# Block-sparse attention and a low-rank mixer with an MLP: two heads' scores side by side, the mask as a product, crossbar transposes, a fixed order

## The chip, the cores and the metric

The kernel runs on one core of a Trainium2 chip. The metric is device microseconds for one execution. Executions are labelled fast or slow by the granted clock and the spread of times, and comparisons use fast runs alone. The profiles are of one execution each. In them PE is TensorE (matmuls), PEld its weight loads, ACT ScalarE, DVE VectorE, POOL GpSimd, and SP the engine that issues most DMAs. A DMA's landing is the time from its issue until all of its data has arrived.

## The reference

Four batches, eight heads, 768 positions, head size 64. Attention sees only some 32-blocks of keys; the result, as 768 x 512 per batch, goes through a rank-32 mixer over the positions and an MLP with 2048 hidden units.

```python
scores = scale * np.matmul(q, k.transpose(0, 1, 3, 2))
mask = np.abs(blk_i - blk_j) <= 1                       # neighbours
mask |= (blk_i == 0) | (blk_j == 0) | (blk_i == n_blocks - 1) | (blk_j == n_blocks - 1)
# ... and three sampled key blocks for each query block
attn = softmax(np.where(mask, scores, -1e9))
x = np.matmul(attn, v)                                  # to (batch, 768, 512)
h = x.transpose(0, 2, 1) @ U @ V
u = x + h.transpose(0, 2, 1)
out = u + np.maximum(u @ w_ch1, 0.0) @ w_ch2
```

## The kernel before

A pair of heads is the unit of work: 16 pairs, four per batch. TensorE transposes q and k. Each head has an augmented q and k of 128 rows: 64 of data and 64 that carry the mask (one-hot blocks on one side, a bias on the other), so that one 128-row product gives masked scores. The exponential runs on ScalarE from PSUM. The MLP of a batch is cut into steps that are dealt out between the score steps of the next batch.

```python
def load_v(b, hp):                       # called at the start of the pair that uses it
    ld = ldpool.tile([P, 2, T, D], FP32, tag="ldv", name="vld")
    nc.sync.dma_start(out=ld, in_=v[b, 2 * hp : 2 * hp + 2].rearrange(...))
    nc.gpsimd.tensor_copy(out=vts[b % 2][:, 2 * hp : 2 * hp + 2, :, 0:D], in_=ld)
# ...
def attn_front(i, st):                   # 12 transposes a pair on TensorE, 4 copies on VectorE
    for s_, aug in zip(st, (qaug, kaug)):
        pstp = pst_tile([P, S], FP16)
        for t in range(T):
            nc.tensor.transpose(out=pstp[:, t * P : (t + 1) * P], in_=..., identity=id16)
        for h in range(2):
            nc.vector.tensor_copy(out=aug[i % NAUG][h][drows[h], :], in_=pstp[drows[h], :])

def attn_scores(i, h, g):                # one head, one key tile: 128 rows, data and mask
    for c in range(2):
        nc.tensor.matmul(psc[:, c, 0:HS], kT[:, g * P : (g + 1) * P],
                         qT[:, c * HS : (c + 1) * HS], start=True, stop=True)
    nc.scalar.activation(out=est..., in_=psc[:, :, 0:HS], func=AF.Exp, scale=0.125)
# ...
def ut(cc):                              # u = x + h, transposed on TensorE, per batch
    # 3 products with the identity and one with the mixer's V, copied by ScalarE
# ...
(load_rest, load_w1, load_mix, load_w2)[hp]()   # weights, in batch one, from GpSimd's queue
```

The scheduler is free to order the instructions of an engine.

The softmax here doesn't subtract the row's maximum and nothing guards it: scores larger than these inputs give would overflow.

## Time and profile before

| | before |
|---|---|
| time, median of two runs | 355.55 us (355.48 to 355.61) |
| TensorE busy, granted clock | 91%, 0.989 |
| batch one (no MLP beside it) | 65.4 us |
| a period with attention and MLP | 80.4 us |
| last MLP alone | 51.5 us |

The lines are shown and read in the prediction below. A windows line has the window, its length, the busy us and count of PE, PEld, DVE, ACT and POOL, the granted clock, the DMA share and GB/s. A line of groups has the place in the code, the engine, what is written from what, the shape, the count, then busy us and mean ns of one, then the idle time in front of it and what ended it. A line number may be that of a helper: after the change all matmuls have the same one, so tile names tell them apart.

### The profile page before, as it was taken

To read this page: it belongs to the slowest core of one execution; us is meant where nothing else is said; L and a number is where in the kernel's file an instruction comes from. 1 tells how busy PE (TensorE), PEld (TensorE's weight loads), DVE (VectorE), ACT (ScalarE), POOL (GpSimd) and SP (SyncE) were. 2 spreads that over 40 slices of the span, in tenths; PEclk is the share of its full clock that TensorE was granted. 3 is DMA by queue.
4 is the path that set the end of the run, shared out by engine and by line. 5 is a ranking of instruction groups with operands and counts; after the bars stand their busy time and mean duration, and the time that the engine had idled before them with its cause. 6 is when DMAs were issued, how large, how long until landed. Compare 5 with 4: busy or idle time off the path is not lost.

```text
span 354.7 us, 6743 instructions
## 1 busy us (share of the span) xinstructions
PE 321.5 (91%) x2803; PEld 189.5 (53%) x2803; DVE 118.5 (33%) x233; ACT 185.5 (52%) x292; POOL 62.5 (18%) x97
## 2 busy tenths in 40 slices
PE   1698882899999999899999999989999999999995
PEld 0356561465756445465756445565756445566442
DVE  3703441034525112324535112325435112244211
ACT  1589993478494431678594431587584432433000
POOL 2519931312303001111202001102101001000000
PEclk9999999799999999999999999999999999999999
DMA  7999999404121111302021211000000011000021
GB/s 236 350 232 229 250 263 291 148 3 133 34 102 55 67 70 52 118 2 89 5 87 27 94 59 61 31 0 3 2 0 2 32 59 61 30 2 0 30 91 59
DMA packets 20874, 30.67 MB, mean 86 GB/s; under 512 B 2444, under 2 KB 17228, under 8 KB 20844
## 3 DMA queue, kind: packets, MB, share of 16 engines
q1 hardware_dynamic: 17184, 25.89, 22.0%
q0 software_dynamic: 3472, 4.24, 7.1%
q8 instruction: 22, 0.36, 0.4%
q10 hardware_dynamic: 188, 0.11, 0.1%
q14 instruction: 8, 0.07, 0.1%
HBM read 28.19 MB, written 6.29 MB: 97 GB/s over the span
## 4 chain that ended last, share of the span: by engine, by line
PE 62%; ACT 16%; DMA 6%; issue 5%; DVE 5%; POOL 5%; ACTq 0%; POOLq 0%; DVEq 0%
PE ps L350 23%; PE ps L333 17%; ACT est L259 13%; PE psc L253 10%; PE ps L273 6%; DMA vld<-in_v_dram 5%; PE ps L238 2%; ACT tT L341 1%; PE ps L348 1%; PE ps L305 1%; DMA small<-small_const 1%; POOL w2t L226 1%; POOL vt_97 L143 1%; POOL vt_98 L143 1%; POOL stqld L133 1%
## 5 line engine op out<-in xcount | busy, mean ns | idle before, releaser
L259 ACT ACTIVATE est<-psc 128x768 f16<-128x768 f32 x192 | 146.4, 826 | 86.0 <-PE psc L253 84.9
L350 PE MATMUL ps<-w2t,tT 128*128 128x512 f16 x384 | 87.3, 379 | 0.0
L333 PEld LDWEIGHTS <-w1t 128*128 128x128 f16 x512 | 48.9, 98 | 33.1 <-DVE q1aug_102 L244 0.7
L343 DVE TENSOR_SCALAR tT<-ps 128x384 f16<-128x384 f32 x64 | 35.7, 558 | 89.5 <-PE ps L333 84.5
L350 PEld LDWEIGHTS <-tT 128*128 128x128 f16 x384 | 37.5, 98 | 43.7
L341 ACT ACTIVATE tT<-ps 128x384 f16<-128x384 f32 x64 | 32.6, 509 | 40.6 <-PE ps L333 29.2
L273 PEld LDWEIGHTS <-est 128*128 128x128 f16 x1152 | 45.6, 98 | 14.6 <-ACT est L259 5.9
L288 POOL CAST xh<-xf 128x384 f16<-128x384 f32 x32 | 16.3, 510 | 197.9 <-DVE xf L282 197.9
L357 DVE TENSOR_TENSOR of<-xf,ps 128x512 f32<-128x512 f32 x24 | 16.5, 688 | 81.1 <-PE ps L350 81.1
L273 PE MATMUL ps<-vt_97,est 128*128 128x65 f16 x576 | 28.3, 196 | 1.8 <-ACT est L259 1.5
L253 PE MATMUL psc<-q0aug_99,k0aug_105 128*128 128x384 f16 x72 | 18.3, 356 | 4.6 <-DVE k0aug_105 L244 2.1
L273 PE MATMUL ps<-vt_98,est 128*128 128x65 f16 x576 | 21.0, 193 | 1.1 <-ACT est L259 0.9
L280 DVE RECIPROCAL rcp<-ps 128x6 f32<-128x6 f32 x32 | 6.2, 194 | 39.3 <-PE ps L273 39.3
L253 PE MATMUL psc<-q1aug_100,k1aug_106 128*128 128x384 f16 x72 | 17.4, 340 | 1.7 <-ACT est L259 1.5
L282 DVE TENSOR_TENSOR xf<-ps,rcp 128x384 f32<-128x384 f32 x32 | 17.8, 558 | 1.2
L253 PE MATMUL psc<-q1aug_104,k1aug_110 128*128 128x384 f16 x60 | 13.5, 325 | 1.6 <-ACT est L259 1.5
L253 PE MATMUL psc<-q1aug_102,k1aug_108 128*128 128x384 f16 x60 | 13.5, 325 | 1.3 <-ACT est L259 1.2
L305 PE MATMUL ps<-xh,Ut 128*128 128x512 f16 x24 | 7.3, 440 | 7.8 <-POOL xh L288 7.8
L253 PE MATMUL psc<-q0aug_103,k0aug_109 128*128 128x384 f16 x60 | 13.5, 325 | 0.9 <-ACT est L259 0.4
L253 PE MATMUL psc<-q0aug_101,k0aug_107 128*128 128x384 f16 x60 | 13.9, 333 | 0.4 <-ACT est L259 0.2
L133 POOL CAST stkld<-kld 128x768 f16<-128x768 f32 x16 | 13.3, 831 | 5.3 <-DMA kld<-in_k_dram 5.3
L133 POOL CAST stqld<-qld 128x768 f16<-128x768 f32 x15 | 12.5, 831 | 7.5 <-issue 5.4
(106 smaller groups left out, 365.9 us busy)
## 6 DMA issues: line engine op xcount, KB each, us to landing
qld<-in_q_dram SPq DMA_DIRECT2D x16, 384.0 KB, 4.7
kld<-in_k_dram SPq DMA_DIRECT2D x16, 384.0 KB, 4.0
vld<-in_v_dram SPq DMA_DIRECT2D x16, 384.0 KB, 3.5
out_dram<-of SPq DMA_DIRECT2D x24, 256.0 KB, 2.0
w1t<-in_moe_w_ch_dram POOLq DMA_DIRECT2D x4, 512.0 KB, 11.0
w2t<-in_moe_w_ch_dram POOLq DMA_DIRECT2D x4, 512.0 KB, 13.2
oh<-onehot_const ACTq DMA_DIRECT2D x1, 96.0 KB, 3.9
q0aug_99<-onehot_const SPq DMA_DIRECT2D x1, 96.0 KB, 4.1
```

Of the source, the lines that this page charges most:

```text
L133: last = eng.tensor_copy(out=st.rearrange("p t h d -> p h t d"), in_=ld)
L253: nc.tensor.matmul(psc[:, c, 0:HS], kT[:, g * P : (g + 1) * P], qT[:, c * HS : (c + 1) * HS], start=True, stop=True,)
L259: nc.scalar.activation(out=est.rearrange("k (c n) -> k c n", c=2), in_=psc[:, :, 0:HS], func=AF.Exp, scale=0.125,)
L273: nc.tensor.matmul(pav[:, j, h, :], ests[h][g][:, sc * P : (sc + 1) * P], vt[:, 2 * hp + h, g, 0 : D + 1], start=(g == 0), stop=(g == T - 1),)
L282: nc.vector.tensor_tensor(out=xs.rearrange("p j (h d) -> p j h d", h=2), in0=pav[:, :, :, 0:D], in1=rcp[:, :, :, None].broadcast_to([P, 3, ...
L288: nc.gpsimd.tensor_copy(out=xh[:, 3 * c : 3 * c + 3, hp * P : (hp + 1) * P], in_=xs)
L305: nc.tensor.matmul(pa, Ut[:, sc, :], xh[:, sc, :], start=(sc == 0), stop=(sc == T - 1))
L333: nc.tensor.matmul(pt, w1t[:, cc, jj * P : (jj + 1) * P], uT[cc][:, c * HS : (c + 1) * HS], start=(cc == 0), stop=(cc == NCC - 1),)
L341: nc.scalar.activation(out=dst, in_=pt, func=AF.Relu)
L343: nc.vector.tensor_scalar_max(out=dst, in0=pt, scalar1=0.0)
L350: nc.tensor.matmul(pch, tT[jj][:, sc * P : (sc + 1) * P], w2t[:, jj, :], start=False, stop=(jj == NJJ - 1),)
L357: nc.vector.tensor_add(out=of, in0=xf[:, sc, :], in1=pch)
```

## The change

The intent is to take work off TensorE, the bound.

1. **Row pairs.** Two heads' data lie in rows 0 to 63 and 64 to 127 of one tile, and two 64-row products run side by side.
2. **Mask.** In batch one it is added by a second 64-row pair of products. From batch two on it is a 0/1 product on VectorE after the exponential.
3. **Mixer per pair** in place of per batch, so that u is ready pair by pair.
4. **Crossbar.** q and k from the third pair on, and all of u, are transposed by DMA; the crossbar stands for this DMA transpose.
5. **Fixed order.** Every engine keeps program order; loads run two pairs ahead; filler (the MLP's steps, put between the score steps) is dealt out by stated costs.

```diff
+def turn_dma(sts):
+    for st, nm in zip(sts, "qk"):
+        tt = qkpool.tile([P, T, P], FP16, tag=nm + "T", name=nm + "T")
+        keep(nc.sync.dma_start_transpose(out=tt, in_=st.rearrange("p t h d -> p (t h d)")))
 ...
+def scores(i, g, c, est, on_pe):
+    for h in range(2):
+        mm(psc[:, h, 0:HS], kT[rows[h], kc], qT[rows[h], qc], True, not on_pe)
+    if on_pe:
+        for h in range(2):
+            mm(psc[:, h, 0:HS], kb[rows[h], kc], oh[rows[h], qc], False, True)
+    keep(nc.scalar.activation(out=est[:, c], in_=psc[:, :, 0:HS], func=AF.Exp, scale=0.125))
+def mask_mul(g, est):
+    keep(nc.vector.tensor_tensor(out=est, in0=est, in1=m01[:, g]...broadcast_to(...), op=ALU.mult))
 ...
+for i in range(HP):                                   # batch one
+    for g in range(T):
+        # scores, values two steps late ...
+        if g == 0: sts[i + 2] = load_qk(i + 2, cast)  # SP load, then GpSimd cast, in order
+        if g == 1: load_v(i + 2)
+        if g == 2:
+            if i == 1: load_w1()
+            if i == 3: load_w2()
+        if g == 3: qkT[i + 1] = turn_pe(sts.pop(i + 1)) if i < 1 else turn_dma(sts.pop(i + 1))
 ...
+FILL = 2.2
+for i in range(HP, NPAIR):                            # batches two to four
+    for g in range(T):                                # a "slot"
+        # two score steps, the mask product of the slot before, then
+        spent += finish_pair(prior, g)                # values in slots 1, 2; mixer in 3, 4, 5
+        if hp == 0 and b > 1 and g == 5: fill.extend(mlp_steps(b - 1))
+        run_fill(FILL - spent)
+        # load_qk in slot 0, load_v in slot 1, turn_dma in slot 3
```

## The prediction

> **What bounds the kernel now.** I read the page first: TensorE is busy for 91% of the span at a granted clock of 0.99, ScalarE for 52%, VectorE for 33%.
>
> ```profile
> PE 321.5 (91%) x2803; PEld 189.5 (53%) x2803; DVE 118.5 (33%) x233; ACT 185.5 (52%) x292; POOL 62.5 (18%) x97
> ```
>
> I then cut the span where the chain of waits changes its character, with the windows view (columns: window, its length, then busy us and count for PE, PEld, DVE, ACT and POOL, granted clock, DMA share, GB/s).
>
> ```profile
> 0.00:65.40 65.40, 42.85 (x459) 27.47 (x460) 22.25 (x49) 41.37 (x55) 32.55 (x50) 0.96 0.98 259
> ...
> 75.50:155.90 80.40, 78.01 (x708) 46.12 (x705) 28.23 (x56) 45.12 (x74) 13.24 (x20) 1.00 0.21 70
> ...
> 303.20:354.70 51.50, 47.31 (x268) 25.01 (x266) 14.44 (x24) 11.02 (x24) 0.00 (x0) 0.99 0.10 36
> ```
>
> There are three kinds of stage. Until 65 us TensorE idles a third of the time and the DMA share is 0.98: batch one's attention has no MLP yet to fill it. Then come three periods of 80.4 us in which attention of one batch and the MLP of the one before share TensorE, busy 97%. Last comes the MLP of batch four alone, 51.5 us.
>
> The chain of waits (start, length, work) gives the rates and batch one's stall:
>
> ```profile
> 43.59 12.76 DMA vld<-in_v_dram
> ...
> 57.27 4.65 DMA vld<-in_v_dram
> ...
> 252.85 2.28 PE ps L273 x72
> ...
> 307.81 20.97 PE ps L333 x128
> ...
> 329.00 3.45 PE ps L350 x16
> 332.67 3.45 PE ps L350 x16
> ```
>
> A matmul's listed duration (326 ns for 384 columns) contains its pipeline, so I use starts. First MLP product: 20.97/128 = 0.164 us. Second: (332.67-329.00)/17 = 0.216 us. Probability times values: 2.28/72 = 0.032 us. In the timeline six transposes take 0.50 us with a tail of about 0.17, so 0.055 each, and four score matmuls take 0.81 us in all, so 0.163 each. The first two lines show batch one waiting 12.76 + 4.65 = 17 us for V, which is on its way beside the weight loads.
>
> The grouped rows price the rest:
>
> ```profile
> L259 ACT ACTIVATE est<-psc 128x768 f16<-128x768 f32 x192 | 146.4, 826 | 86.0 <-PE psc L253 84.9
> ...
> L343 DVE TENSOR_SCALAR tT<-ps 128x384 f16<-128x384 f32 x64 | 35.7, 558 | 89.5 <-PE ps L333 84.5
> ...
> L282 DVE TENSOR_TENSOR xf<-ps,rcp 128x384 f32<-128x384 f32 x32 | 17.8, 558 | 1.2
> ```
>
> Back to back an exponential costs 146.4/192 = 0.763 us, and it spends 85 us waiting for scores: ScalarE isn't the bound outside batch one.
>
> [...] Only start-up has a change: after the two 24-row mask matmuls (0.82 us from 8.14) the 128-row transposes start 0.11 us later than 384 columns at the cold rate (0.32 us) allow. That is weak evidence for some 0.1 us. [...]
>
> **The change part by part**, TensorE time per batch in the steady stage. Before: 96 scores x 0.163 = 15.6; 288 values x 0.032 = 9.1; 48 transposes of q and k x 0.055 = 2.6; six 512-column mixer products 1.3; the u-transposes, 24 x 0.055 + 8 x 0.163 = 2.6; 128 x 0.163 = 20.8; 102 x 0.216 = 22.0. Sum 74.0 of the 80.4.
> - Scores: a head needs only 64 rows once the mask rows leave the product. Two heads side by side make 48 steps of 0.163 in place of 96: -7.8. In batch one the mask is still added by a second 64-row pair, so nothing is saved there.
> - The crossbar takes all but two q/k transposes and all u-transposes off TensorE: -2.6 and -2.6. The mixer becomes 24 + 24 products of 128 columns, 2.6, in place of 1.3 plus the six in the second MLP product, 1.3: nothing.
> - Sum 61.0 per batch: 13.0 less, 39 over three batches.
> - VectorE: 24 mask products of 1536 elements, [...] +23.0. Mixer adds 8 x 0.56 and four small casts, +5.7. Gone are 16 copies of 0.55 and one cast, -9.5. From 28.2 it goes to about 47: beside TensorE's 61, off the path.
> - ScalarE loses eight u-copies of about 0.55: from 45.1 to about 41.
> - The fixed order deals out 2.2 us of filler, mixer and value work per slot of two score steps, so a slot is about 2.2 + 2 x 0.163 = 2.53 us on TensorE against 2 x 0.763 + about 1.3 x 0.51 = 2.2 on ScalarE.
>
> Now the time, stage by stage. **Batch one:** first exponential at about 12 us as before (12.61), 48 x 0.8 = 38.4, since ScalarE binds there. V is fetched two pairs ahead, so the 17 us wait goes; but the crossbar transposes of pairs three and five are queued just behind w1 and w2 loads (11 and 13 us to landing each), for which I add 6. End at 57. **72 slots:** scores 144 x 0.163 = 23.4; values of 11 pairs 25.1; mixer 8.0; MLP 3 x 41.5 less about 9 that the slots don't reach = 115.5. Sum 172. Two mode switches a slot at 0.1 (chosen from the weak evidence): 14.4. Counting the code's stated costs (41.7 a batch against 2.2 a slot), the filler is empty in about five slots, which then last the exponentials' 1.55: +4.5. Twice the MLP of a batch is queued in the very slot in which its last transpose is issued, so TensorE waits for add, cast and crossbar, about 4 each (add and cast 1.1 from rows of that kind, a small DMA 2 to 3 by the landing times of before): +8. The opening of batch two +2, plain gaps as before (80.4 - 78.0 a batch) +7. Sum 208. **Tail:** last pair's values and mixer 3.0, left-over MLP 9, the last MLP 41.5, output 3.7: 57. In all 57 + 208 + 57 = 322 us, against 355.6.
>
> **Rivals.** *The row pairs don't overlap, or the switches are dear.* Without overlap +0.163 x (144 + 96) = +39, less what batch one hides behind ScalarE: about 350, no gain. With switches of 0.2 us instead of 0.1: +14, 336. [...] *The crossbar is the new wait:* if a 192 KB transpose takes 6 us or more, two of them no longer fit in the three slots (7.6 us) before their use: +1 to 3 us a pair, 335 to 350. DMA is idle (share 0.2) after batch one, which speaks against; in batch one it is the likeliest loss. *Everything is hidden anyway:* with free switches and quick transposes, 300.
>
> **Range and chances.** The range 303 to 341 runs from free switches and transposes to 0.2 us a switch with a slow crossbar. To land above 348 both TensorE terms must fail together. Chances: faster 0.93, same 0.05, slower 0.02.
>
> **What would show it.** Right: steady batches of 65 to 69 us; two score matmuls starting within some ns of each other; mask products near 0.96 us; batch one over near 57; TensorE waits of about 4 us near the start of batches three and four; a last stage of about 57. The prediction would be wrong most of all if score pairs start 0.16 us apart, if gaps of 0.2 us stand at each change between 64 and 128 rows, if mask products last 1.8 us, or if TensorE waits for transposes in every pair.

## The result

| | before | changed |
|---|---|---|
| median of two runs | 355.55 us (355.48 to 355.61) | 375.14 us (373.28 to 377.01) |
| granted TensorE clock | 0.989 | 0.904 |

The ratio is 1.054, with a 95% interval of 1.041 to 1.067: the changed kernel is slower by 5%, where 322 us and a gain were forecast. A ratio here is the mean time of one kernel's fast runs over that of the other's of the same rounds, so it is not quite the ratio of the medians that I quote.

The page of the changed kernel, busy times and the slices of TensorE, its clock and the DMA (40 slices of 9.4 us):

```profile
PE 307.9 (82%) x2759; PEld 155.8 (42%) x2759; DVE 173.8 (46%) x298; ACT 175.8 (47%) x258; POOL 89.9 (24%) x129
...
PE   1985078850799999795699997987899999999995
...
PEclk9999559585589999999599999998899999999999
DMA  7816944299390044438340906264802011210011
```

TensorE's busy time fell only from 321.5 to 307.9 us, and it now idles for 67 us. There are two holes in batch one, and the clock is at half in and after them. The windows view, cut where batches begin:

```profile
0.00:93.00 93.00, 51.84 (x555) 24.74 (x555) 21.86 (x51) 38.73 (x50) 29.91 (x49) 0.80 0.67 145
93.00:167.00 74.00, 69.41 (x578) 33.83 (x580) 43.33 (x69) 42.95 (x64) 19.54 (x26) 0.89 0.41 112
167.00:241.10 74.10, 63.64 (x627) 33.30 (x628) 44.10 (x73) 42.99 (x64) 21.36 (x29) 0.93 0.44 111
241.10:317.10 76.00, 69.73 (x658) 35.37 (x658) 46.02 (x75) 43.28 (x64) 16.18 (x23) 0.96 0.33 79
317.10:375.20 58.10, 53.28 (x349) 28.59 (x346) 18.53 (x33) 7.86 (x16) 2.91 (x5) 1.00 0.14 48
```

Batch one takes 93.0 us, where 57 was predicted (+36). The 72 slots take 224.1, where 208 was (+16). The tail takes 58, where 57 was. That is the whole miss of 53 us. The waits view of the changed kernel (who waited for whom, total us, times, longest) names three new waits of TensorE, for kT (k transposed), xh (x in float16, which the mixer reads) and uT (u transposed), and the wait of GpSimd that stands behind the one for xh:

```profile
POOL qst L140 <- DMA qld<-in_q_dram: 33.7, 8, 6.1
...
PE psc L104 <- DMA kT<-kst: 28.4, 3, 14.5
...
PE pa L104 <- POOL xh L331: 15.1, 15, 3.6
PE pt L104 <- DMA uT<-uh: 7.8, 3, 4.0
```

**The wait for k.** The timeline of SP, the DMA-issuing engine (start, duration of the issue, what):

```profile
30.48 1.32 SPq L378 DMA_TRANSPOSE uT<-uh  x1
31.85 1.78 SPq L181 DMA_TRANSPOSE qT<-qst  x1
33.68 10.20 SPq L181 DMA_TRANSPOSE kT<-kst  x1
43.92 0.58 SPq L132 DMA_DIRECT2D qld<-in_q_dram  x1
```

The w1 load was issued at 30.40. The transpose of k behind it lands 14.5 us after its issue; even the issue takes 10.20 us, and the loads of the pair after next stand behind it. The DMA view from 38 to 42 us, in the midst of the w1 load (queue, packets, MB, share of 16 engines; q0 has the weights, q1 what SP issued):

```profile
q0 software_dynamic: 218, 0.77, 95.1%
q1 hardware_dynamic: 219, 0.05, 11.0%
```

The same from 86 to 90 us, in the w2 load:

```profile
q0 software_dynamic: 629, 0.63, 92.2%
q1 hardware_dynamic: 626, 0.15, 29.6%
```

And from 60 to 64 us, where three transposes run with no weights beside them:

```profile
q1 hardware_dynamic: 2400, 0.59, 65.5%
```

In the two windows beside a load both queues moved the same number of packets, 218 to 219 and 629 to 626, as if they took turns. A packet of the weight load holds 3.5 KB (0.77 MB/218) or 1.0 KB; a packet of the transpose holds 0.24 KB. So the transpose crawls there at one packet for each of the other's, and the load with the smaller packets lets through three times as much of it (0.15 against 0.05 MB; 0.59 MB with no load beside it). Not every microsecond is so even: from 34 to 36 us the view has 82 packets against 534, which nothing here explains. The trace shows what equal counts cost the side with the small packets: the transpose of k behind w1, 192 KB, lands in 14.5 us, where the quickest of k takes 2.6 and of u 2.5. The hold of the issue shows in the w2 load too: 4.31 us for the transpose of k issued at 78.81, where that of pair four took 1.24. In the prediction I looked up only how long the loads take.

**The clock.** From 40 to 50 us TensorE is busy for 1.83 us and the granted clock is 0.50, and it stays low for part of the next 60 us (0.67 from 50 to 110 us). After the second hole too it is 0.50, from 93 to 98 us. So the holes of 14.5 and 12.6 us go with half clock. But the clock also fell after far shorter pauses: from 62.0 to 65.4 us TensorE's longest is 1.36 us, a wait for k, and half clock follows for 10 us.

```profile
62.00:65.40 3.40, 2.04 (x26) 0.86 (x25) 1.29 (x4) 1.61 (x3) 0.00 (x0) 1.00 0.61 123
65.40:75.60 10.20, 9.02 (x74) 4.11 (x74) 3.66 (x8) 4.39 (x7) 4.57 (x8) 0.50 0.28 103
```

A wait of 1.47 us before 156.41 is followed by half clock too (0.50 from 157.6 to 160.9 us); one of 1.72 us before 232.99 is not (1.00 from 233 to 238 us). So these traces give no length of pause from which the clock falls. The first two slots after the first hole, those of pair three, last 4.3 and 3.4 us; those of pair two lasted 3.2 and 1.6.

**The wait for xh.** GpSimd's timeline in pair eight (start, duration, what, idle before it):

```profile
153.15 0.83 POOL L140 CAST qst<-qld 128x768 f16<-128x768 f32 x1 [5.99 <-DMA qld<-in_q_dram]
154.36 0.83 POOL L140 CAST kst<-kld 128x768 f16<-128x768 f32 x1 [0.38 <-DMA kld<-in_k_dram]
155.13 1.23 POOL L331 CAST xh<-xs 128x384 f16<-128x384 f32 x1
```

In the fixed order the cast of q for a later pair stands ahead of the cast of x, which the mixer needs now. It idles 5.99 us for its load, which was itself late: SP issued it at 149.70, behind an output store that had to wait for VectorE. The first product of the mixer then starts at 156.41, after 1.47 us of idle TensorE, and such waits come again in pairs nine, twelve and thirteen.

```profile
156.41 0.33 PE L104 MATMUL pa<-xh,Ut 128*128 128x128 f16 x3 [1.47 <-POOL xh L331]
```

**What was as forecast.** The timeline of PE in batch one:

```profile
30.12 0.33 PE L104 MATMUL psc<-oh,kb 64*128 64x384 f16 x2
30.38 0.35 PE L104 MATMUL pav<-vt,est 128*128 128x65 f16 x6
30.66 0.34 PE L104 MATMUL psc<-qT,kT 64*128 64x384 f16 x2
30.84 0.33 PE L104 MATMUL psc<-oh,kb 64*128 64x384 f16 x2
```

Two products of 384 columns take the time of one, and the next pair starts 0.18 us later: the row pairs overlap. From the 64-row pair at 30.12 to the 128-row product at 30.38 are 0.26 us, 0.10 more than the 0.16 that 384 columns take. Over all 67 changes each way between 110 and 320 us the median cost is 0.098 us into 64 rows and 0.095 out, computed from start to start, less the columns at that rate. The groups that answer to those of before:

```profile
L301 ACT ACTIVATE est<-psc 128x768 f16<-128x768 f32 x192 | 145.3, 809 | 108.9 <-PE psc L104 108.7
...
L308 DVE TENSOR_TENSOR est<-est,m 128x1536 f16<-128x1536 f16 x72 | 71.8, 997 | 0.7 <-ACT est L301 0.6
```

A mask product takes 997 ns for 1536 elements, where 960 was forecast. At the pace of VectorE's float32 rows from PSUM in the kernel before (384 elements in 558 ns, 512 in 688, so 1.02 ns an element and 168 ns besides) I estimate 1.7 us.

### The profile page after: what moved, and what is told of

Read it like the earlier page. It is cut to its first block, busy times and chain, and to the rows that moved or that the text cites.

```text
span 375.2 us, 6642 instructions
## 1 busy us (share of the span) xinstructions
PE 307.9 (82%) x2759; PEld 155.8 (42%) x2759; DVE 173.8 (46%) x298; ACT 175.8 (47%) x258; POOL 89.9 (24%) x129
## 5 line engine op out<-in xcount | busy, mean ns | idle before, releaser
L104 PE MATMUL pt<-uT,w1t 128*128 128x384 f16 x512 | 96.0, 341 | 7.8 <-DMA uT<-uh 7.8
L104 PE MATMUL pch<-w2t,tT 128*128 128x512 f16 x384 | 92.1, 388 | 0.0
L104 PE MATMUL psc<-qT,kT 64*128 64x384 f16 x384 | 58.3, 355 | 29.9 <-DMA kT<-kst 28.4
L308 DVE TENSOR_TENSOR est<-est,m 128x1536 f16<-128x1536 f16 x72 | 71.8, 997 | 0.7 <-ACT est L301 0.6
L402 ACT ACTIVATE tT<-pt 128x384 f16<-128x384 f32 x64 | 31.5, 492 | 55.7 <-PE pt L104 55.2
L404 DVE TENSOR_SCALAR tT<-pt 128x384 f16<-128x384 f32 x64 | 35.6, 557 | 46.6 <-PE pt L104 45.7
L104 PE MATMUL pav<-vt,est 128*128 128x65 f16 x1152 | 50.5, 197 | 0.0
L373 POOL CAST uh<-xf 128x384 f16<-128x384 f32 x32 | 20.9, 656 | 98.7 <-DVE xf L369 57.9
L331 POOL CAST xh<-xs 128x384 f16<-128x384 f32 x32 | 20.4, 636 | 71.4 <-DVE xs L324 67.9
L321 DVE RECIPROCAL rcp<-pav 128x6 f32<-128x6 f32 x32 | 6.2, 195 | 40.8 <-PE pav L104 40.6
L140 POOL CAST qst<-qld 128x768 f16<-128x768 f32 x15 | 12.7, 846 | 51.8 <-DMA qld<-in_q_dram 33.7
L104 PE MATMUL pa<-xh,Ut 128*128 128x128 f16 x96 | 11.0, 239 | 15.4 <-POOL xh L331 15.1
L104 PE MATMUL psc<-oh,kb 64*128 64x384 f16 x96 | 19.7, 385 | 0.5 <-ACT kb L242 0.5
```

The costliest lines, as they stand in the source:

```text
L104: nc.tensor.matmul(out, lhsT, rhs, start=start, stop=stop, skip_group_check=loose)
L140: keep(cast[nm].tensor_copy(out=st.rearrange("p t h d -> p h t d"), in_=ld))
L308: nc.vector.tensor_tensor(out=est, in0=est, in1=m01[:, g].rearrange("p (c n) -> p c n", c=2)[:, :, None, :] .broadcast_to([P, 2, 2, HS]), ...
L321: keep(nc.vector.reciprocal(out=rcp, in_=pav[:, :, :, D]))
L331: keep(nc.gpsimd.tensor_copy(out=xh[:, 3 * c : 3 * c + 3, :], in_=x3))
L373: keep(nc.gpsimd.tensor_copy(out=uh[:, 3 * c : 3 * c + 3, :], in_=u3))
```

## The experiments

All kernels were correct. "Before" was run beside each, 354 to 358 us. There are four runs of each kernel (two of the changed one), and times are medians of them; the ratios leave out one slow run each of E2 and E11 (the medians of their fast runs are 348.8 and 323.0). The two runs of the changed kernel lie 3.7 us apart, so a difference from it carries some 2 us of doubt.

| kernel | us | ratio to before (95%) |
|---|---|---|
| changed | 375.1 | 1.054 (1.041 to 1.067) |
| E1: q, k of pairs one to five on TensorE | 353.2 | 0.993 (0.987 to 0.998) |
| E2: weight loads apart | 349.4 | 0.980 (0.975 to 0.985) |
| E3: casts late | 364.6 | 1.026 (1.023 to 1.030) |
| E4: filler 1.85 and 2.1 | 371.8 | 1.044 (1.038 to 1.049) |
| E5: E1 + E3 + E4 | 334.4 | 0.942 (0.935 to 0.948) |
| E6: E5, mask on TensorE | 346.7 | 0.973 (0.968 to 0.978) |
| E7: E5, all q, k on TensorE | 341.0 | 0.958 (0.953 to 0.962) |
| E8: changed, order free | 355.9 | 1.002 (0.998 to 1.006) |
| E9: E5 + E2 | 327.1 | 0.919 (0.914 to 0.924) |
| E10: E9, order free | 348.8 | 0.981 (0.977 to 0.986) |
| E11: E9, casts last, filler 1.8 and 2.15 | 323.4 | 0.908 (0.903 to 0.912) |

### E1: transposes of batch one back on TensorE

```diff
-qkT[i + 1] = turn_pe(sts.pop(i + 1)) if i < 1 else turn_dma(sts.pop(i + 1))
+qkT[i + 1] = turn_pe(sts.pop(i + 1)) if i < HP else turn_dma(sts.pop(i + 1))
```

> Only batch one is changed: q and k of its pairs (and of pair five) are transposed on TensorE again, the u transposes stay on the crossbar. Theory A (the crossbar's 256-byte packets take turns with the weight loads' packets of 1 to 4 KB, so transposes last as long as the weight load): TensorE's waits of 14.5 and 12.6 us for k go, and with them the half clock after them; batch two starts near 60 us in place of 93, total near 342 us. Rival B (whatever queues behind the weight loads waits, so the wait moves to the q, k and v loads): the fourth or fifth pair then waits 10 us or more for a load, total 355 to 375.

353.2 us, 22 less. Both long waits for k are gone and batch two starts at 66.6 us in place of 93.0. It isn't the 60 us expected, and the total is 11 us above theory A's 342, because waits of other kinds are left in batch one: TensorE waits 2.2 us at 51.3 for xh, whose cast stands on GpSimd behind a cast of q that waits for its load; the granted clock falls to 0.54 from 50 to 60 us; and the first four slots of pair four last 4.9, 3.4, 3.0 and 4.0 us. TensorE's longest wait for a transpose from 48 to 90 us is 2.1 us, for u of pair four. The wait of 10 us that rival B asks for isn't seen; GpSimd's longest wait for a load there is 5.6 us.

### E2: weight loads apart from the transposes

```diff
-if g == 2:
-    if i == 1: load_w1()
-    if i == 3: load_w2()
+if g == 2 and i == 0: load_w1()
+if g == 0 and i >= 2: load_w2(i - 2)          # a quarter each
 ...                                            # and the same in pairs five and six
```

> The crossbar does what it did, but the weight loads are issued where few transposes are in flight: w1 in pair one, w2 in four pieces at the start of pairs three to six. Theory A: the k transposes land within 6 us, no wait over 3 us in batch one, total 340 to 350 us. Rival C (two 192 KB crossbar transposes in a row are too slow for a short pair by themselves, with or without weights): waits of 8 us or more before pairs three and five stay, total above 365 us.

349.4 us, 26 less, with the crossbar doing all that it did. The time to landing of the k transposes (minimum, median, maximum of 14), first in the changed kernel:

```profile
DMA to landing us min/median/max: 2.6/5.8/14.5
```

In E2:

```profile
DMA to landing us min/median/max: 2.6/4.9/6.7
```

The longest wait of TensorE for k is 2.5 us; the longest landing is a little over the 6 us expected. (The profiled execution is one labelled slow, 352.4 us, the other three are 346.8 to 350.0; I use it for the landings and this wait alone.) Theory A holds and C falls: the crossbar is quick enough by itself; what cost the time here was running for long beside a load with larger packets (14.5 us to landing there, 6.7 at most in E2). E1 and E2 take away either side of the same collision and gain about the same.

### E3: casts after what the mixer needs

```diff
-sts[i + 2] = load_qk(i + 2, cast)             # slot 0: load and cast; after stores and filler
-load_v(i + 2)                                  # slot 1
+sts[i + 2] = load_qk(i + 2, cast, casts)      # at the start of slot 0: load alone
+load_v(i + 2, casts)
+if g == 4:
+    while casts: casts.popleft()()             # the casts, in slot 4
```

> Batch one's waits stay. q, k and v of the pair after next are requested at the start of a pair before anything else, and their casts stand in GpSimd's fixed order in slot five, after the casts of x that the mixer needs. Theory D (in the fixed order a cast that waits for its load holds the cast of x behind it, and TensorE waits for that one): TensorE's 12 us of waits for xh in pairs eight to thirteen fall below 2 us, total 8 to 11 us less, near 365 us. [...]

(The expectation counts slots from one, the code from zero.)

364.6 us, 10.6 less, in the waits view:

```profile
POOL qst L141 <- DMA qld<-in_q_dram: 1.0, 1, 1.0
...
PE pa L104 <- POOL xh L335: 6.1, 10, 1.4
```

GpSimd's wait for q falls from 33.7 to 1.0 us, TensorE's for xh from 15.1 to 6.1. In batches two to four those over 0.45 us sum to 2.5; below 2 was expected. The total came as expected. Theory D holds. The mask products aren't the main cause of these waits: they are all still there. They do lengthen the casts (686 ns beside them, 509 without, in E5 and E6). The waits for u, which this edit was not meant for, grow from 7.8 to 10.7 us.

### E4: less filler in a slot

```diff
-run_fill(FILL - spent)                         # 2.2
+run_fill((1.85 if i < 9 else 2.1) - spent)
```

(A plain 1.85 could not be built: too much filler was left over, and a tile of an older batch was still held by it.)

> Batch one's waits stay. One number is changed: the filler dealt out per slot is 1.85 us up to pair nine and 2.1 us after, in place of 2.2, so that filler of the batch before is left when the next batch's is queued. Theory E (TensorE waits 2.9 and 4.0 us for the last u transpose because the filler has run out, and the clock falls to half after it): both waits vanish, slots of 9.2 and 8.2 us become 2.5, total 8 to 12 us less, near 365 us. Rival: the work only moves to the last stage, total the same.

371.8 us, 3.3 less, which isn't clear of the noise (1.044, 1.038 to 1.049, against 1.054, 1.041 to 1.067), where 8 to 12 were expected. The waits for the last u transpose fall from 7.8 to 1.5 us and the slots of 9.2 and 8.2 us become 2.4 and 3.3, as theory E has it. But the waits for xh grow from 15.1 to 19.9 us and the slot with the mixer's first product takes up to 8.3 us. So waits of another kind grew where these went.

### E5: the three together

> The three edits together: q and k of pairs one to five transposed on TensorE, casts late, filler 1.85 and 2.1. If the three causes are separate (crossbar beside weights -22 us measured, xh casts behind loads -10.6, filler -3.3 measured), the total is 375 - 36 = 339 us; if the filler's gain was masked by the xh waits that grew in its place, some 6 us more comes off: 330 to 335. Rival: the gains overlap and the total stays above 345.

334.4 us, 40.8 less than the changed kernel; the three alone sum to 36. So the edits help each other by some 5 us, and the total is in the range of the second expectation. That it is E4's gain, hidden behind the waits that E3 takes away, fits E4's longer waits for xh and E3's longer ones for u, but no run of two of the edits shows it. This version beats both kernels: the change's arithmetic is worth its price once these waits are gone.

### E6: the mask on TensorE in all batches

```diff
-scores(i, g, c, est, False)
-if g > 0: mask_mul(g - 1, ests[g - 1])
+scores(i, g, c, est, True)
```

> The three edits, with the mask added on TensorE by a second 64-row pair in all batches and no product on VectorE. If the row pairs and the product are worth what the prediction said (144 steps of 0.163 us), this is 20 to 25 us slower than the three edits alone. Rival: VectorE's product holds up TensorE elsewhere [...] and gives half of it back: 5 to 12 us slower.

346.7 us, 12.4 more than E5: between the two expectations, nearer the rival's. TensorE has 144 steps of 0.163 = 23.5 us more to do, so half of what the product saves is lost again. A part is seen in the windows view from 93 to 263 us; E5 first, then E6:

```profile
93.00:263.00 170.00, 164.33 (x1664) 86.15 (x1662) 119.09 (x193) 112.06 (x167) 56.49 (x70) 0.99 0.47 108
```

```profile
93.00:263.00 170.00, 170.00 (x1802) 90.61 (x1801) 57.46 (x119) 106.55 (x156) 40.96 (x67) 1.00 0.40 107
```

With VectorE at 57 us in place of 119 and GpSimd at 41 in place of 56, TensorE doesn't idle at all; in E5 it idles 5.7 us. Over all 72 slots it idles 15.7 us in E5 and 8.7 in E6, so some 7 of the 11 us lost are idle time; the rest I have not settled.

GpSimd's share is a result of its own. Its casts of x, E5 first, then E6:

```profile
L335 POOL CAST xh<-xs 128x384 f16<-128x384 f32 x32 | 21.9, 686 | 100.5 <-DVE xs L328 100.5
```

```profile
L335 POOL CAST xh<-xs 128x384 f16<-128x384 f32 x32 | 16.2, 509 | 124.9 <-DVE xs L328 124.9
```

Without the mask products a cast is back at the 510 ns of the kernel before, so it is they that cost it some 177 ns; by what means the traces don't show.

### E7: q and k of all pairs on TensorE

```diff
-qkT[i + 1] = turn_dma(sts.pop(i + 1))          # batches two to four
+qkT[i + 1] = turn_pe(sts.pop(i + 1))
```

> The three edits, with q and k of all pairs transposed on TensorE, so that the crossbar turns u only. If the crossbar is free outside batch one, TensorE's 11 x 12 x 0.055 = 7 us more show in full: 6 to 8 us slower than the three edits alone. Rival: the crossbar's transposes hold up loads on the in-order queue also in the later batches; then it is the same or faster.

341.0 us, 6.7 more: the 11 x 12 x 0.055 = 7 us of transposes show in full. Outside batch one the crossbar is free, as predicted.

### E8 and E10: the scheduler free to order

```diff
-keep = tc.keep_in_program_order
+keep = lambda x: x
```

> The changed kernel with the scheduler free to order the instructions, all else as it is. If the fixed order is what makes queue heads wait (xh casts behind casts that wait for loads, loads behind stores), the scheduler orders around them and 8 to 15 us come off: 360 to 367. Rival: the fixed order is worth its price, since the scheduler puts filler elsewhere than where TensorE needs it; then 375 to 390. Batch one's two waits of 12 to 15 us for the crossbar should stay in either case.

355.9 us, 19 less, more than expected, and the part of my expectation that both long waits stay was wrong. The free scheduler issues the first of w1 at 3.47 us and the last of w2 at 40.69. Two transposes of that time still land after 11.2 and 13.6 us, but TensorE doesn't wait for them, and the later ones have no weight load to collide with. One wait of 14.8 us, for xh, remains, and its reason is theory D's; the load that holds GpSimd there is one of k that was issued beside w2 and landed after 11.2 us. GpSimd's timeline:

```profile
39.92 0.83 POOL L140 CAST kst<-kld 128x768 f16<-128x768 f32 x1 [7.47 <-DMA kld<-in_k_dram]
40.69 0.75 POOL L270 DMA_DIRECT2D w2t<-in_moe_w_ch_dram  x1
41.43 0.96 POOL L331 CAST xh<-xs 128x384 f16<-128x384 f32 x2
```

> The version with all edits and the weights apart (327.1 us), with the scheduler free to order. If the fixed order's harm was the two things already mended, a free order is no better: 325 to 340. Rival: order still costs some us at the start of batch two, and this is faster by 3 us or more.

With the same freedom the mended version gets slower, 348.8 against 327.1 us, more than either expectation allowed: the scheduler again moves the weight loads to the front, and TensorE once waits 10.2 us for a cast of x. So the order isn't good or bad by being fixed. Fixed as it came, it cost 19 us against a free one; fixed with casts, loads and weights in their places, it gains 22.

### E9 and E11: the best version

E9 is E5 with E2's edit; E11 is E9 with the edit shown below.

> The three edits plus the weight loads apart from the transposes (w1 in pair one, w2 in four pieces). In the kernel with TensorE transposes alone the u transposes of pairs three and four still waited 14 us in the queue behind w2, and the clock fell to half from 50 to 60 us and 70 to 80 us. If that is the weights' doing, batch two starts 5 to 10 us earlier and the total is 5 to 10 us below the three edits alone. Rival: the low clock comes from batch one being short of TensorE work; then it is within 3 us.

327.1 us, 7.3 below E5, as expected. Batch two starts only 2.0 us earlier (61.6 for 63.5), not 5 to 10; most of the rest is gained in its third slot, which takes 6.4 us in place of 12.3. There E5 waited 7.0 us for u of pair four: its transpose, issued at 69.46 beside the w2 load, landed 8.3 us later. From 68 to 72 us the weight queue had 418 packets (0.43 MB) to 419 of the other (0.62 MB). At 1.5 KB each these 419 aren't the transpose's but the q, k and v loads ahead of it in its own queue, slowed beside w2 at the same one for one; only 17 of all packets then were under 512 B, as its own are. In E9 it lands after 2.7 us and the wait is 1.2 us.

One sentence of the expectation was a misreading of mine: no u transpose waited some 14 us in a queue behind w2. The timeline had put two issues on one line, from the start of the first to the end of the second. By themselves they took 1.3 and 1.7 us. The late landing, not a held issue, is what E9 takes away.

> The version with all edits and the weights apart, with the casts of the loads one slot later, behind the cast of u, and filler 1.8 and 2.15 us. In the version before, the last u transpose of batch two still came 2.0 us late and the two slots after it took 5.0 and 3.6 us. If the casts in front of it were the reason, these become 2.5 and 3.0 us: 3 to 4 us less, 323 to 324. Rival: the crossbar itself is that slow behind the loads; then the same within 1 us.

```diff
-run_fill((1.85 if i < 9 else 2.1) - spent)
-if g == 4:
+run_fill((1.8 if i < 9 else 2.15) - spent)
+if g == 5:
     while casts: casts.popleft()()
```

323.4 us (three fast runs of 321.4 to 323.8, median 323.0), 3.7 less, as expected: the slots of 5.0 and 3.6 us are 3.1 and 2.3. Two things were changed in one run, so their shares aren't known. Its windows for batches two and three:

```profile
63.80:128.40 64.60, 58.12 (x538) 28.88 (x536) 44.24 (x71) 42.82 (x64) 23.57 (x29) 0.92 0.54 116
128.40:191.90 63.50, 62.94 (x640) 33.06 (x640) 45.16 (x73) 42.99 (x64) 21.45 (x28) 1.00 0.60 134
```

This is 9.2% below the kernel before, and near the 322 us that had been forecast for the change.

## Why the prediction was wrong

- **Row pairs overlap: right.** Starts lie 3 ns apart at the median of pairs, and the products of a pair take the time of one. It was an assumption of mine: the kernel before has no 64-row product to show it.
- **A mode switch (between 64 and 128 rows) costs about 0.1 us: right.** 0.098 and 0.095 us measured; the weak evidence from start-up was good. Its "cold rate" is that of start-up, where six transposes take 0.62 us from start to start (from 14.19 us), against 0.34 later (from 254.97 us).
- **The mask product: right**, 997 ns against 960, though the kernel before has no such product to show the pace that I assumed. VectorE at 43 to 46 us a batch against 47, ScalarE at 43 against 41.
- **Half of the product's gain is lost again: missed.** It was priced at its TensorE time alone; E6 shows that 12.4 of 23.5 us remain.
- **"for which I add 6": the step that failed first.** The collision of crossbar and weight loads was named, as batch one's likeliest loss, and sized by the loads' landing times, with nothing on how a transpose shares the DMA engines. It was two waits of 14.5 and 12.6 us, plus slots at half clock. E1 and E2 put it at 22 to 26 us. E9 shows 7.3 us more where u and the loads ahead of it meet w2.
- **"48 x 0.8 = 38.4, since ScalarE binds there": too small as well.** Even in E9, with no long wait left in batch one, 49.6 us pass from the first exponential (11.97) to batch two (61.56), and ScalarE waits 13.1 us of them for scores. Slots that hold the mixer's steps last up to 3.7 us, where two exponentials take 1.4 to 1.6.
- **"plain gaps as before" (+7 in the sum): the second step that failed.** I carried over the gaps of a freely ordered kernel to a fixed order, and didn't follow GpSimd's and SP's queues. E3 puts the casts that wait at their head at 10.6 us.
- **The wait for the last u transpose: right in place and size, too small in effect.** 2.9 and 4.0 us against 4 each; but the slots that hold them took 9.2 and 8.2 us, since the clock fell after the pause (0.59 from 180 to 190 us). E4 and E5 put it at 8 us at most (3.3, and the 5 that the edits gain together).
- **Tail: right**, 58 against 57.

The terms measured by removal, 40.8 (E5) + 7.3 (E9) + 3.7 (E11) = 51.8 us, come near the miss of 53. That E11 meets the forecast is in part luck. Its three stages:

```profile
0.00:63.80 63.80, 48.26 (x593) 24.81 (x595) 24.84 (x53) 38.31 (x50) 27.25 (x45) 1.00 0.75 193
63.80:257.20 193.40, 185.81 (x1827) 95.86 (x1826) 136.93 (x218) 128.81 (x192) 63.41 (x80) 0.97 0.50 114
257.20:321.70 64.50, 60.16 (x380) 31.76 (x378) 19.87 (x35) 7.84 (x16) 2.88 (x5) 1.00 0.15 52
```

Forecast were 57, 208 and 57: batch one and the tail are some 7 us longer each and the slots 15 shorter, the tail and the slots in part because less filler is dealt out. The chance of 0.93 for faster was too sure, because it counted only rivals of the arithmetic and one of the crossbar by itself, and none of one transfer beside another. "To land above 348 both TensorE terms must fail together" was wrong for the same reason: neither failed, and it took 375. It also contradicts the prediction's own crossbar rival, which went up to 350. One reading was loose: the "three periods of 80.4 us" run from 65.4 to 303.2 us, 79.3 each; little rests on it.

## What to carry to other kernels

Before a transfer is moved to DMA, list what else is in flight then and compare packet sizes: here two queues moved equal numbers of packets (218 to 219, 629 to 626), and the one with packets of 0.24 KB moved 0.05 MB in 4 us beside packets of 3.5 KB, 0.15 beside 1.0 KB and 0.59 with no load beside it. In a fixed order, look at each in-order queue for an instruction that waits for something slow in front of one that something else needs now; move loads to the front and what waits for them to the back. A pause of TensorE can cost more than its length, since the clock comes back late: 7.0 us after the work did in the first hole (0.50 from 48.2 to 55.2 us).
